# Attention beside a gated feed-forward block on one core: the row maxima reach the query rows by VectorE and DRAM instead of TensorE, and a tanh moves one mark forward

## The chip, the cores and the metric

The kernel runs on 1 core of one Trainium2 chip. The metric is device time in microseconds (us), the median of several runs. Five engines work side by side, each with its own in-order instruction stream: TensorE (PE in the profile, with its weight loads listed apart as PEld), VectorE (DVE), ScalarE (ACT), GpSimd (POOL) and SyncE (SP), whose queue issues all of this kernel's DMAs. PE writes its sums into PSUM banks; DVE and ACT read them there.

## The reference, cut to what matters

```python
def _A_ref(x, wqkv, wo):                       # S 2048, D 576, H 32, Dh 18
    q, k, v = ...
    scores = jnp.einsum("bhqd,bhkd->bhqk", q, k) * (Dh ** -0.5)
    p = softmax(scores, axis=-1)
    o = jnp.einsum("bhqk,bhkd->bhqd", p, v)
    return o.transpose(0, 2, 1, 3).reshape(B, S, D) @ wo

def _B_ref(x, w_gate, w_up, w_down):           # F 4608
    return (gelu(x @ w_gate, approximate=True) * (x @ w_up)) @ w_down

xn = layernorm(x, axis=-1, eps=1e-5)
out = x + _A_ref(xn, wqkv, wo) * silu(_B_ref(xn, w_gate, w_up, w_down))
```

Everything is float32. The softmax subtracts the maximum of each query's row, and the change is about how that maximum gets to where it is subtracted.

## The kernel before, in words

A prologue normalizes x, computes q, k and v and writes them to DRAM, each number as a rounded high part and a low remainder. The main part is one long hand-written PE order (PE alone is scheduled by hand; the order on the other engines and on the DMA queue is a planner's, which keeps to the hand-made order where the code asks for it). An epilogue projects the attention output and combines.

**Sections.** The main part consists of 144 sections (`section`). Section n computes one 128-wide slice of gate and up (`gate_up`: `pg` and `pu`, 27 pairs of matmuls that run side by side on the two 64-row halves of PE), and between those pairs the attention's matmuls are spread. The first ten sections (`FIRST`) lead in; the 128 sections of `ATT` carry the attention. After the matmuls of a section come, on odd attention sections, the products with the values (`values`), and on even ones the down projection of the slices two sections back (`half_downs`). After 36 sections a block of 512 tokens is complete and the next block's x is loaded (a block change).

**Attention units.** A unit is 4 heads by 512 queries, 32 units in all, 4 sections each. Two matmuls serve a unit's scores. `max_mm` computes scores with queries on the partitions (`pm`), and a `TENSOR_REDUCE` on DVE keeps each row's maximum (L701). It runs 40 slots, that is 5 sections, ahead of `score_mm`, which computes the scores again with keys on the partitions (`pe`), already with the maximum subtracted, and ACT takes the exponential (L736). The subtraction costs no operation of its own: the query tiles (`QS`, rows of 64 per head) have spare rows from `MROW` (54) on that meet rows of ones in the key tiles, and the negated maximum, as a high and a low part, is written into two of those rows by DMA. So the maximum, which DVE has with queries on partitions, has to become a row along the free axis. That is what the change touches:

- `max_neg` (L703 on, called when a unit's last maximum is done, in every fourth section, always an even one): the four parts of each maximum are reduced and negated (`nm`, L706), and split into high and low (L708, L709) in a constant tile `m2_ident`, which also holds an identity.
- `max_end` (L711 on): called in the middle of that section's down projection (`half_downs`, `middle`). PE multiplies the two 64-row halves of the parts with the identity (L717), which transposes them into two PSUM banks (tags `m` and `f`); ACT copies them out (`mr`, L720); eight DMAs on the SP queue write the rows of the query tiles (L725).
- The unit's first `score_mm` comes two sections after `max_neg`.

**The down projection in halves.** `half_downs` makes 8 sums of 128x288 (`py`, k = 0 to 7), each of 12 matmuls, 6 on the lower and 6 on the upper 64 rows of PE. Two lanes run side by side, 48 steps of two matmuls: lane 1 does k = 0 to 7 in order, lane 0 does k = 6, 7, then 0 to 5. So sum k = 0 is begun in steps 0 to 5 on lane 1 and ended in steps 12 to 17 on lane 0, and so on. When lane 1 has finished its half of a sum (k = 0 to 5, every six steps), a tiny ACT instruction (`mark`, L471) follows it, and lane 0's half waits for the mark. A finished sum is added to `Y` by DVE (`add_down`, L455), which frees its PSUM bank. Banks are handed out by tag in turn, `bank("mmsmfmss"[k])`, with 2 of tag `f`, 3 of `m` and 3 of `s`: sum k = 5, begun at step 30 on lane 1, is the fourth of tag `m` and takes the bank of k = 0. The bank of k = 4 is that of `pg`.

**The activation.** `activate` makes the gated value of a section: ACT squares `pg` (L430), DVE forms the polynomial (L431), then `times` (ACT copies `pu`, L435; DVE multiplies by `pg`, L438) and `rest` (ACT's tanh, L441; DVE's product, L444). In sections with a down projection `times` and `rest` are popped out of a list by it: `times` behind the mark of k = 0, `rest` behind the mark of k = 2. `finish` then splits the result on POOL (`hh`, `hl`, L108 and L110), and POOL goes on to split the next weights.

**The DMA queue.** SP issues the keys (`KS`, L667, 12 DMAs a section), the weights (L128), the values, the query rows and the small transfers of the softmax sums in the planner's order; an issue that has to wait holds up all behind it.

Of the kernel before, what the change touches and what calls it, by code (L numbers as in the profile page):

```python
# [8 lines left out]
F32 = mybir.dt.float32  # L9
F32R = mybir.dt.float32r  # L10
AF = mybir.ActivationFunctionType
# [30 lines left out]
FIRST = (0, 0, 4, 4, 4, 4, 6, 6, 6, 6)  # L42
ATT = range(len(FIRST), len(FIRST) + NU * NA)
MROW = 3 * DH
MH = 32
MW = 72
NK = KT + 1
BANKS = {"f": 2, "m": 3, "s": 3}
EPS = 1e-5
# [5 lines left out]
def f(ap):  # L55
    return ap.bitcast(F32)
# [13 lines left out]
def kernel(ctx: ExitStack, tc: tile.TileContext, x, wqkv, wo, w_gate, w_up, w_down, out):  # L70
# [14 lines left out]
    rT = dram.tile([H, S], F32, name="rT")  # L85
    oN = dram.tile([D, S], F32, name="oN")
    ys = dram.tile([S - TB, D], F32, name="ys")
    zq = dram.tile([HR - MROW, TB], F32, name="zq")
    xhs = [dram.tile([2, D, TB], F32, name=f"xhs{b}") for b in range(NB)]

    m2_ident = const.tile([P, 2 * MH + HR], F32R, name="m2_ident")
    M2 = m2_ident[:, 0:2 * MH].rearrange("p (i c) -> p i c", c=MH)
    identr = m2_ident[:, 2 * MH:2 * MH + HR]
    all_t = slice(0, TB)

    def after(what, before):
# [62 lines left out]
    with tc.tile_pool(name="pro", bufs=1) as pro, tc.tile_pool(name="pps", bufs=1, space=PSUM) as pps:  # L159
        ident = pro.tile([P, P], F32, name="ident")  # L160
        make_identity(nc, ident)
        for a in (0, HR):
            nc.gpsimd.tensor_copy(identr[a:a + HR], ident[a:a + HR, a:a + HR])

        def load_rest(c0, n, keep=lambda i: i):

# [234 lines left out]
    def kept(i):  # L401

        if FF["keep"]:
            tc.keep_in_program_order(i)
        return i
# [21 lines left out]
    def activate(pg, pu, early):  # L427

        t1 = ffn.tile([P, TB], F32, name="t1", bufs=2)
        kept(nc.scalar.activation(t1, pg, AF.Square))  # L430
        kept(nc.vector.scalar_tensor_tensor(t1, t1, 1.0 / GC, pg, op0=ALU.add, op1=ALU.mult))  # L431
        t2 = ffn.tile([P, TB], F32, name="t2", bufs=1) if early else None

        def times(behind=None):
            one = nc.scalar.activation(t2, pu, AF.Copy)  # L435
            if behind:
                no_sync(one, behind, "a mark first")
            nc.vector.tensor_tensor(t2, t2, pg, op=ALU.mult)  # L438

        def rest(behind=None):  # L440
            tanh = kept(nc.scalar.activation(t1, t1, AF.Tanh, scale=GC * GS))  # L441
            if behind:
                no_sync(tanh, behind, "a mark first")
            kept(nc.vector.scalar_tensor_tensor(t1, t1, 1.0, t2 if early else pg, op0=ALU.add, op1=ALU.mult))  # L444
            if not early:
                kept(nc.vector.tensor_tensor(t1, t1, pu, op=ALU.mult))

        return t1, [times, rest] if early else [rest]

    def add_down(b, r, py, Y, j, c):  # L450
        yy = Y[:, j, 288 * c:288 * c + 288]
        if r == 0:
            nc.vector.tensor_copy(yy, py)
        else:
            kept(nc.vector.tensor_tensor(yy, py, yy, op=ALU.add))  # L455
        if b == NB - 1 and r == NR - 1:
            FF["final"](Y, j, c)

    DOWN = [(a, w, g) for g in range(G) for a, w in ((0, 0), (0, 1), (1, 0))]

# [11 lines left out]
        after(it, one)  # L472
        return it

    def half_downs(b, r, hs, wd, Y, middle=None):

        m = len(DOWN)
        sums = [(j, c) for j in range(TB // P) for c in range(2)]  # L480
        low = len(sums) - 2
        pys, seen = {}, {}

        def downs_of(a, ks):
            for k in ks:
                for i in range(m):
                    def step(k=k, i=i):
                        j, c = sums[k]
                        fresh = k not in pys
                        if fresh:  # L490
                            pys[k] = bank("mmsmfmss"[k])
                        begun = a if k < low else 1 - a
                        one = down_product(pys[k], hs, wd, j, c, i, slice(HR * a, HR * a + HR), fresh,
                                           begun == 0 and i == m - 1)
                        if begun == 0 and i == 0 and k in seen:
                            after(one, seen[k])
                        if i == m - 1:
                            if begun == 0:
                                add_down(b, r, pys[k], Y, j, c)
                            elif a == 1:  # L500
                                seen[k] = behind(one)
                                if k in (0, 2) and FF["rest"]:
                                    FF["rest"].pop(0)(seen[k])
                    yield step

        n = range(len(sums))
        rows = [*downs_of(0, n[low:]), *downs_of(0, n[:low])], [*downs_of(1, n)]
        for i, both in enumerate(zip(*rows, strict=True)):
            for half in both if i < low * m + m else both[::-1]:
                half()  # L510
            if middle and i == (low - 1) * m + 1:
                middle()

    def down(b, r, hs, wd, Y, js, once):
        last = len(DOWN) - 1
        if once:
            if js[0] == 0:
                half_downs(b, r, hs, wd, Y, FF.pop("middle", None))
        else:
            for j in js:  # L520
                for c in range(2):
                    py = bank("sf"[c if b == NB - 1 and r == NR - 1 else 0])
                    for i in range(len(DOWN)):
                        down_product(py, hs, wd, j, c, i, start=(i == 0), stop=(i == last))
                    add_down(b, r, py, Y, j, c)
        if b < NB - 1 and r == NR - 1:
            for j in js:
                kept(nc.sync.dma_start(ys[b * TB + j * P:b * TB + (j + 1) * P, :], Y[:, j]))
# [117 lines left out]
    with tc.tile_pool(name="att", bufs=1, reuse_waits="tile") as att:  # L646
        VS = [att.tile([P, VC * VW + 32 - DH - 1], F32, name=f"VS{i}") for i in range(VB)]
        for i, kk in enumerate(KS):
            for r in range(2):
                (nc.vector, nc.gpsimd)[i % 2].memset(f(kk[r]), 1.0)  # L650
        nc.vector.memset(f(M2), 0.0)
        for vv in VS:
            nc.vector.memset(vv[:, VC * VW:], 0.0)

# [22 lines left out]
        QS, MX, ACC, PT, NM, DEN, PIECE = {}, {}, {}, {}, {}, {}, {}  # L677

        def load_q(u, rs=(0, 1)):
            j, g = divmod(u, NQ)  # L680
# [21 lines left out]

        def max_neg(u, keep=lambda i: i):  # L703

            nm = att.tile([P, 4 * QD], F32, name="nm", bufs=1)
            keep(nc.vector.tensor_reduce(nm, MX[u].rearrange("p a t c -> p (a t) c"), axis=AX.X, op=ALU.max, negate=True))  # L706
            NM[u], m2 = u, M2
            nc.vector.tensor_copy(m2[:, 0, 0:4 * QD], nm)  # L708
            nc.vector.tensor_tensor(m2[:, 1, 0:4 * QD], nm, f(m2)[:, 0, 0:4 * QD], op=ALU.subtract)  # L709

        def max_end(u, tags="mf"):  # L711

            NM.pop(u)
            pms = [ps.tile([P, TB], F32, name="pm", tag=tag, bufs=BANKS[tag])[0:MW, 0:HR] for tag in tags]
            for a, pm in enumerate(pms):
                rr = slice(HR * a, HR * a + HR)
                nc.tensor.matmul(pm, m2_ident[rr, 0:MW], identr[rr], start=True, stop=True)  # L717
            mr = att.tile([P, TB // 2], F32, name="mr", tag="piece", bufs=2)[:, 0:P]
            for a, pm in enumerate(pms):
                nc.scalar.activation(mr[0:2 * MH, HR * a:HR * a + HR], pm[0:2 * MH], AF.Copy)  # L720
            for a in range(QD):
                for i in range(2):
                    row = 64 * (a % 2) + MROW + i
                    c = MH * i + 4 * a
                    nc.sync.dma_start(f(QS[u, a // 2])[row:row + 1, :], mr[c:c + 4, :])  # L725

        def score_mm(u, i, a, tag="s"):

# [89 lines left out]
        for n, m in enumerate(FIRST):  # L818
            none = [lambda: None]
            lead = [lambda s=s: lead_pair(s) for s in range(slot, slot + m)]  # L820
            if 0 in NM:
                lead.insert(1, lambda: max_end(0, "ms"))
            section((n == 2) * 5 * none + lead + (m > 0 and n != 2) * none, "s" if n == 1 else "f", lead_raw)
            if slot + m >= NS > slot:
                max_neg(0, tc.keep_in_program_order)
            slot += m
            while n > 1 and chunk < KB and chunk * SLOTS <= slot + SLOTS:
                load_k(chunk, tc.keep_in_program_order)
                chunk += 1
            if n == 3:  # L830
                load_q(1)
            if n >= len(FIRST) - 2:
                load_v(n - len(FIRST) + 2)
            downs()
            finish(cut=split_ap)
        for n in range(NU * NA):
# [13 lines left out]
            um, im = divmod(s0 + LEAD + SLOTS, NS)  # L850
            if im == 0 and um <= NU:
                max_neg(um - 1)
                FF["middle"] = lambda u=um - 1: max_end(u)
            if i % 2:
                for kt in range((i - 1) * VC, (i + 1) * VC):
                    values(u, kt)
# [192 lines left out]
```

## Time and profile before

| | us |
|---|---|
| median of 3 runs | 2559.11 (2557.44 to 2561.36) |
| the profiled execution's own time | 2559.35 |
| its span, first to last instruction | 2557.3 |
| PE busy with matmuls | 2544.7 |
| DVE busy | 1948.9 |
| ACT busy | 1563.7 |
| POOL busy | 1321.8 |
| DVE's maxima (L701), 2048 times | 1250.0 |
| DVE's sums into Y (L455), 544 times | 228.8 |

The busy time of an engine counts time in which at least one of its instructions runs; matmuls overlap, since each starts before the one ahead of it has drained. The time of 2559.35 us has 2.05 us around the span. In views by time, a row gives the start, the duration, the engine, the source line, the operation, output and inputs, the shape, the count where equal rows are merged, and in brackets the idle time before it with what ended it.

### The profile page before, as it was taken

The numbers are of one execution on the slowest core, as the hardware profiler recorded it, in microseconds if no ns is written. First come the engines' busy times: TensorE is split into PE (matmuls) and PEld (weight loads), VectorE is DVE, ScalarE is ACT, GpSimd is POOL, SyncE is SP. The second block draws the span as 40 slices with busy tenths as digits, with TensorE's granted clock in tenths as the row PEclk, the third lists the DMA queues.
The fourth block names the chain that finished last, engine by engine and source line by source line (L and its number), as shares of the span: only waits on it lengthen the run. The fifth ranks groups of instructions, "written<-read, shape, count | busy, mean of one in ns | idle before, by whom it ended". The sixth has DMA issues, their size and how long they took to land.

```text
span 2557.3 us, 63358 instructions
## 1 busy us (share of the span) xinstructions
PE 2544.7 (100%) x24038; PEld 1977.7 (77%) x24038; DVE 1948.9 (76%) x3468; ACT 1563.7 (61%) x3114; POOL 1321.8 (52%) x1449
## 2 busy tenths in 40 slices
PE   9999999999999999999999999999999999999999
PEld 8888877777777777777777777777777777777798
DVE  5316978888888888888888888888888888886277
ACT  3223467666667666667666667666666666676612
POOL 2117645555565555444556554554446555555575
PEclk9999999999999999999999999999999999999999
DMA  8876343444464444444455443444446444443483
GB/s 267 270 238 161 94 106 92 108 105 110 109 155 118 106 103 111 112 112 111 109 122 141 115 108 101 109 104 109 109 99 159 111 109 109 111 107 99 113 245 105
DMA packets 391006, 324.98 MB, mean 127 GB/s; under 512 B 108704, under 2 KB 301504, under 8 KB 390704
## 3 DMA queue, kind: packets, MB, share of 16 engines
q1 hardware_dynamic: 390704, 320.94, 48.6%
q8 instruction: 191, 3.13, 0.5%
q14 instruction: 111, 0.91, 0.1%
HBM read 266.10 MB, written 54.18 MB: 125 GB/s over the span
## 4 chain that ended last, share of the span: by engine, by line
PE 95%; DVE 2%; ACT 2%; DMA 1%; issue 0%; POOL 0%; SPq 0%; ACTq 0%; DVEq 0%; POOLq 0%
PE pg L417 31%; PE acc L770 17%; PE py L466 16%; PE pm L700 9%; PE pe L735 9%; PE po L184 7%; PE pu L417 3%; PE po L909 2%; DVE t L444 1%; ACT pT L736 1%; ACT t L441 1%; DVE Y L455 0%; DMA xd<-xhs 0%; DVE mx L701 0%; PE pt L245 0%; PE pm L717 0%
## 5 line engine op out<-in xcount | busy, mean ns | idle before, releaser
L736 ACT ACTIVATE pT<-pe 128x512 f32<-128x512 f32 x2048 | 1151.3, 598 | 370.3 <-PE pm L700 266.2
L701 DVE TENSOR_REDUCE mx<-pm 128x1 f32<-128x512 f32 x2048 | 1250.0, 680 | 151.9 <-PE pm L700 149.3
L417 PE MATMUL pu<-xd,wh 64*128 64x512 f32 x2592 | 929.3, 390 | 0.6 <-POOL xd L148 0.5
L417 PE MATMUL pg<-xd,wh 64*128 64x512 f32 x2592 | 928.7, 390 | 0.0
L700 PE MATMUL pm<-KS,q 64*128 64x512 f32 x2048 | 782.5, 387 | 0.0
L735 PE MATMUL pe<-q,KS 64*128 64x512 f32 x2048 | 776.8, 387 | 0.0
L417 PEld LDWEIGHTS pg<-xd,wh 64*128 64x128 f32 x2592 | 476.4, 184 | 127.5 <-issue 26.1
L417 PE MATMUL pu<-xd,wl 64*128 64x512 f32 x1296 | 501.5, 387 | 0.0
L417 PE MATMUL pg<-xd,wl 64*128 64x512 f32 x1296 | 501.4, 387 | 0.0
L417 PEld LDWEIGHTS pu<-xd,wh 64*128 64x128 f32 x2592 | 476.8, 184 | 4.2 <-POOL xd L148 1.5
L770 PE MATMUL acc<-pT,VS 128*32 128x512 f32 x4096 | 452.8, 594 | 0.0
L110 POOL TENSOR_TENSOR wl<-raw,wh 128x384 fp32r<-128x384 f32 x432 | 433.9, 1018 | 13.7
L700 PEld LDWEIGHTS pm<-KS,q 64*128 64x128 f32 x2048 | 374.3, 184 | 35.0 <-DVE mx L701 3.8
L735 PEld LDWEIGHTS pe<-q,KS 64*128 64x128 f32 x2048 | 370.1, 184 | 27.1
L108 POOL TENSOR_SCALAR hh<-t 128x512 fp32r<-128x512 f32 x128 | 79.2, 619 | 579.8 <-DVE t L444 565.7
L770 PEld LDWEIGHTS acc<-pT,VS 128*32 128x32 f32 x4096 | 127.3, 110 | 289.9 <-issue 278.6
L466 PE MATMUL py<-dh,hl 64*128 64x288 f32 (+1 forms) x2160 | 344.2, 295 | 0.0
L466 PE MATMUL py<-dh,hh 64*128 64x288 f32 (+1 forms) x2160 | 343.0, 292 | 0.3
L466 PE MATMUL py<-dl,hh 64*128 64x288 f32 (+1 forms) x2160 | 341.5, 292 | 0.0
L108 POOL TENSOR_SCALAR wh<-raw 128x384 fp32r<-128x384 f32 x432 | 217.7, 516 | 130.2 <-PE pu L417 79.2
L455 DVE TENSOR_TENSOR Y<-py,Y 128x288 f32<-128x288 f32 x544 | 228.8, 452 | 58.6 <-PE py L466 51.9
L417 PEld LDWEIGHTS pg<-xd,wl 64*128 64x128 f32 x1296 | 238.6, 184 | 38.2
(123 smaller groups left out, 3067.0 us busy)
## 6 DMA issues: line engine op xcount, KB each, us to landing
KS<-qk SPq DMA_DIRECT2D x1536, 36.0 KB
raw<-in_B_w_gate_dram SPq DMA_DIRECT2D x144, 288.0 KB
raw<-in_B_w_up_dram SPq DMA_DIRECT2D x144, 288.0 KB
raw<-in_B_w_down_dram SPq DMA_DIRECT2D x67, 576.0 KB
VS<-vs SPq DMA_DIRECT2D x128, 152.0 KB
qk<-t SPq DMA_DIRECT2D x72, 256.0 KB
q<-qk SPq DMA_DIRECT2D x384, 36.0 KB
xx<-in_A_x_dram SPq DMA_DIRECT2D x32, 288.0 KB
```

The lines of the kernel that those rows point to most:

```text
L108: first = nc.gpsimd.tensor_scalar(hi, raw, 1.0, 1.0, op0=ALU.mult, op1=ALU.mult)
L110: low_part[:] = [keep(nc.gpsimd.tensor_tensor(lo, raw, f(hi), op=ALU.subtract))]
L184: nc.tensor.matmul(o, st, m, start=(i == 0), stop=(i == len(terms) - 1))
L417: nc.tensor.matmul(o, w[1 + wp][k][rr, c, :], xd[xp][k][rr, c, :], start=(i == 0), stop=(i == len(terms) - 1))
L455: kept(nc.vector.tensor_tensor(yy, py, yy, op=ALU.add))
L466: return nc.tensor.matmul(py, hs[g][a][rr, j * P:(j + 1) * P], wd[w][rr, g, 288 * c:288 * c + 288], start=start, stop=stop)
L700: nc.tensor.matmul(pm, QS[u, r][rr, t * P:(t + 1) * P], KS[(u * NA + c) % KB][r][rr, :], start=True, stop=True)
L701: nc.vector.tensor_reduce(MX[u][:, 2 * r + a, t, c:c + 1], pm, axis=AX.X, op=ALU.max)
L735: nc.tensor.matmul(pe, KS[(u * NA + c) % KB][r][rr, t * P:(t + 1) * P], QS[u, r][rr, :], start=True, stop=True)
L736: nc.scalar.activation(PT[u, kt][:, 2 * r + a, :], pe, AF.Exp, scale=SCALE)
L770: nc.tensor.matmul(ACC[u][32 * a:32 * a + 32, :], VS[(u * NA + c) % VB][:, v:v + 32], pt[:, a, :], start=first, stop=last, skip_group_chec ...
L909: nc.tensor.matmul(po, parts_of(b, j)[x_][:, k, :], OW[w][c][k], start=(i == 0), stop=(i == len(OUT) - 1))
```

## The change

The maxima's parts no longer pass through PE and ACT. `max_neg` puts high and low part side by side into a 128x32 tile `m2`, DVE transposes it in squares of 32 (`m2t`), and one DMA stores it to a DRAM tile `mT` of the unit. `max_rows` reads it back with eight DMAs, one for each row, each in 16 pieces of 32 numbers. It is called in the section after `max_neg`, but the planner puts its DMAs behind the twelve key loads of the section of `max_neg`. `max_end`, its 64 matmuls and 64 ACT copies, the identity and the place in the middle of the down projection go away; the transposes add 32 instructions on DVE and the stores 32 DMAs.

In the planned order, `mT`'s store stands between the eighth and the ninth key load, and the eight row loads right behind the twelfth. On DVE the transpose stands between L431 and L438.

The second part: `rest` is popped behind the mark of k = 1 instead of k = 2, except where the down projection is a block's last (`r == NR - 1`). There it stays at k = 2, and its DVE product is kept behind the sum of k = 0. Elsewhere the DVE order becomes L431, (transpose,) L438, L444, and then the eight sums; before, the sum of k = 0 stood ahead of L444.

```diff
-MH = 32
-MW = 72
+MH = 16
+SQ = 32
...
+    mT = [dram.tile([P, SQ], F32, name=f"mT{u}") for u in range(NU)]
...
-    m2_ident = const.tile([P, 2 * MH + HR], F32R, name="m2_ident")
-    M2 = m2_ident[:, 0:2 * MH].rearrange("p (i c) -> p i c", c=MH)
-    identr = m2_ident[:, 2 * MH:2 * MH + HR]
...
-        def rest(behind=None):
+        def rest(behind=None, evicted=None):
             tanh = kept(nc.scalar.activation(t1, t1, AF.Tanh, scale=GC * GS))
             if behind:
                 no_sync(tanh, behind, "a mark first")
-            kept(nc.vector.scalar_tensor_tensor(t1, t1, 1.0, t2 if early else pg, op0=ALU.add, op1=ALU.mult))
+            one = kept(nc.vector.scalar_tensor_tensor(t1, t1, 1.0, t2 if early else pg, op0=ALU.add, op1=ALU.mult))
+            if evicted:
+                no_sync(one, evicted, "a finished sum first")
...
-    def half_downs(b, r, hs, wd, Y, middle=None):
+    def half_downs(b, r, hs, wd, Y):
...
-        pys, seen = {}, {}
+        pys, seen, evicted = {}, {}, None
+        late = 2 if r == NR - 1 else 1
...
                             if begun == 0:
-                                add_down(b, r, pys[k], Y, j, c)
+                                evicted = add_down(b, r, pys[k], Y, j, c)
                             elif a == 1:
                                 seen[k] = behind(one)
-                                if k in (0, 2) and FF["rest"]:
-                                    FF["rest"].pop(0)(seen[k])
+                                if k in (0, late) and FF["rest"]:
+                                    FF["rest"].pop(0)(seen[k], evicted if k == 2 else None)
...
-            if middle and i == (low - 1) * m + 1:
-                middle()
...
-            nm = att.tile([P, 4 * QD], F32, name="nm", bufs=1)
+            nm = att.tile([P, MH], F32, name="nm", bufs=1)
+            m2 = att.tile([P, 2 * MH], F32R, name="m2", bufs=1)
+            m2t = att.tile([P, SQ], F32, name="m2t", bufs=1)
             keep(nc.vector.tensor_reduce(nm, MX[u].rearrange("p a t c -> p (a t) c"), axis=AX.X, op=ALU.max, negate=True))
-            NM[u], m2 = u, M2
-            nc.vector.tensor_copy(m2[:, 0, 0:4 * QD], nm)
-            nc.vector.tensor_tensor(m2[:, 1, 0:4 * QD], nm, f(m2)[:, 0, 0:4 * QD], op=ALU.subtract)
-
-        def max_end(u, tags="mf"):
-
-            NM.pop(u)
-            pms = [ps.tile([P, TB], F32, name="pm", tag=tag, bufs=BANKS[tag])[0:MW, 0:HR] for tag in tags]
-            for a, pm in enumerate(pms):
-                rr = slice(HR * a, HR * a + HR)
-                nc.tensor.matmul(pm, m2_ident[rr, 0:MW], identr[rr], start=True, stop=True)
-            mr = att.tile([P, TB // 2], F32, name="mr", tag="piece", bufs=2)[:, 0:P]
-            for a, pm in enumerate(pms):
-                nc.scalar.activation(mr[0:2 * MH, HR * a:HR * a + HR], pm[0:2 * MH], AF.Copy)
+            nc.vector.tensor_copy(m2[:, 0:MH], nm)
+            nc.vector.tensor_tensor(m2[:, MH:2 * MH], nm, f(m2)[:, 0:MH], op=ALU.subtract)
+            nc.vector.transpose(m2t, f(m2))
+            nc.sync.dma_start(mT[u], m2t)
+
+        def max_rows(u):
+
+            parts = mT[u].rearrange("(b i a t) r -> i a t b r", i=2, a=QD, t=4)
             for a in range(QD):
                 for i in range(2):
-                    row = 64 * (a % 2) + MROW + i
-                    c = MH * i + 4 * a
-                    nc.sync.dma_start(f(QS[u, a // 2])[row:row + 1, :], mr[c:c + 4, :])
+                    row = HR * (a % 2) + MROW + i
+                    nc.sync.dma_start(f(QS[u, a // 2])[row:row + 1, :].rearrange("o (t b r) -> o t b r", t=4, r=SQ),
+                                      parts[i:i + 1, a])
...
             if slot + m >= NS > slot:
                 max_neg(0, tc.keep_in_program_order)
+                max_rows(0)
...
                 max_neg(um - 1)
-                FF["middle"] = lambda u=um - 1: max_end(u)
+                at(n + 1, 0, max_rows, um - 1)
```

More of the change, by code (lines that the diff above doesn't have):

```diff
@@ L161 @@
         make_identity(nc, ident)
-        for a in (0, HR):
-            nc.gpsimd.tensor_copy(identr[a:a + HR], ident[a:a + HR, a:a + HR])
         def load_rest(c0, n, keep=lambda i: i):
@@ L432, in activate, with times @@
         t2 = ffn.tile([P, TB], F32, name="t2", bufs=1) if early else None
-        def times(behind=None):
+        def times(behind=None, _=None):
             one = nc.scalar.activation(t2, pu, AF.Copy)
@@ L452, in add_down @@
         if r == 0:
-            nc.vector.tensor_copy(yy, py)
+            one = nc.vector.tensor_copy(yy, py)
         else:
-            kept(nc.vector.tensor_tensor(yy, py, yy, op=ALU.add))
+            one = kept(nc.vector.tensor_tensor(yy, py, yy, op=ALU.add))
         if b == NB - 1 and r == NR - 1:
             FF["final"](Y, j, c)
+        return one
     DOWN = [(a, w, g) for g in range(G) for a, w in ((0, 0), (0, 1), (1, 0))]
@@ L487, in step @@
                     def step(k=k, i=i):
+                        nonlocal evicted
                         j, c = sums[k]
@@ L517, in down @@
             if js[0] == 0:
-                half_downs(b, r, hs, wd, Y, FF.pop("middle", None))
+                half_downs(b, r, hs, wd, Y)
         else:
@@ L650 @@
                 (nc.vector, nc.gpsimd)[i % 2].memset(f(kk[r]), 1.0)
-        nc.vector.memset(f(M2), 0.0)
         for vv in VS:
@@ L675, in load_v @@
                                   vs[c * TB:(c + 1) * TB, QD * g:QD * (g + 1), :].rearrange("(t p) h d -> p t (h d)", p=P))
-        QS, MX, ACC, PT, NM, DEN, PIECE = {}, {}, {}, {}, {}, {}, {}
+        QS, MX, ACC, PT, DEN, PIECE = {}, {}, {}, {}, {}, {}
         def load_q(u, rs=(0, 1)):
@@ L820 @@
             lead = [lambda s=s: lead_pair(s) for s in range(slot, slot + m)]
-            if 0 in NM:
-                lead.insert(1, lambda: max_end(0, "ms"))
             section((n == 2) * 5 * none + lead + (m > 0 and n != 2) * none, "s" if n == 1 else "f", lead_raw)
```

## The prediction

> **What bounds the kernel now.** First the page: busy times, and the chain that ended last.
>
> ```profile
> span 2557.3 us, 63358 instructions
> PE 2544.7 (100%) x24038; PEld 1977.7 (77%) x24038; DVE 1948.9 (76%) x3468; ACT 1563.7 (61%) x3114; POOL 1321.8 (52%) x1449
> PE 95%; DVE 2%; ACT 2%; DMA 1%; issue 0%; POOL 0%; SPq 0%; ACTq 0%; DVEq 0%; POOLq 0%
> ```
>
> PE is busy all the time and is 95% of the chain. Only two things can then move the end: PE instructions that go away, and moments in which PE stands still. DVE, ACT, POOL and SP matter only where they make PE wait. So next: does PE stand still around the removed matmuls? The view of the tile `m_ident`, and of the marks:
>
> ```profile
> L717 PEld LDWEIGHTS pm<-m_ident x64: 136/136/137, 288.8 to 2352.3; 64*72 64x72 f32 x64
> L709 DVE TENSOR_TENSOR m_ident<-nm,m_ident x32: 174/176/1211, 287.5 to 2349.1; 128x16 fp32r<-128x16 f32 x32
>   DVE Y L455: 13.1, 33
> L471 ACT ACTIVATE mark<-mark 128x1 f32<-128x1 f32 x378 | 76.9, 203 | 117.6 <-PE py L466 107.0
> ```
>
> There are 64 loads, a pair for each of 32 units, and before them PE sat idle for 13.1 us, waiting for a sum of DVE: the transposes want two PSUM banks in the middle of a down projection, and the `m` bank is still waiting to be added to `Y`. The 378 marks are 6 for each of 63 down projections in halves; 31 of these hold a transpose (the first unit's stands in the lead), 32 do not. Now PE's timeline through one of each kind, first the one with:
>
> ```profile
> 1210.85 0.29 PE L466 MATMUL py<-dh,hh 64*128 64x288 f32 x2
> ...
> 1215.38 0.25 PE L717 MATMUL pm<-m_ident 64*72 64x64 f32 x2
> ...
> 1217.68 0.39 PE L417 MATMUL pg<-xd,wh 64*128 64x512 f32 x1
> ```
> ```profile
> 1177.72 0.29 PE L466 MATMUL py<-dh,hh 64*128 64x288 f32 x2
> ...
> 1184.08 0.39 PE L417 MATMUL pg<-xd,wh 64*128 64x512 f32 x1
> ```
>
> From the first sum to the next section's first matmul it is 6.83 us with the transpose and 6.36 without: 0.47 us for each.
>
> **The change, part by part.** *The matmuls of L717 go.* 31 x 0.47 = 14.6 us of PE time. The pair in the lead stands between matmuls that need no bank of it, and I count it at nothing. The 64 copies on ACT (L720) go too, which PE never waited for. At least the idle 13.1 us is gone, at most 14.6 plus a few tenths.
>
> *DVE gets a transpose, and the first sum moves behind the tanh's product.* This is where something can be given back, since DVE's first sum frees the bank of k = 5. The three views of the section at 1210.85, DVE, ACT and the weight load of step 30 (1210.85 plus 30 steps of 0.13 us is its matmul at 1214.82, the load stands one step ahead):
>
> ```profile
> 1211.97 0.17 DVE L708 CAST m_ident<-nm 128x16 fp32r<-128x16 f32 x1
> 1212.18 0.18 DVE L709 TENSOR_TENSOR m_ident<-nm,m_ident 128x16 fp32r<-128x16 f32 x1
> 1212.28 0.68 DVE L431 SCALAR_TENSOR_TENSOR t<-t,pg 128x512 f32<-128x512 f32 x1
> 1212.87 0.68 DVE L438 TENSOR_TENSOR t<-t,pg 128x512 f32<-128x512 f32 x1
> 1213.47 0.45 DVE L455 TENSOR_TENSOR Y<-py,Y 128x288 f32<-128x288 f32 x1
> 1214.27 0.69 DVE L444 SCALAR_TENSOR_TENSOR t<-t,t 128x512 f32<-128x512 f32 x1 [0.35 <-ACT t L441]
> 1214.88 0.81 DVE L455 TENSOR_TENSOR Y<-py,Y 128x288 f32<-128x288 f32 x2
> ```
> ```profile
> 1212.70 0.20 ACT L471 ACTIVATE mark<-mark 128x1 f32<-128x1 f32 x1
> 1213.51 0.20 ACT L471 ACTIVATE mark<-mark 128x1 f32<-128x1 f32 x1 [0.62 <-PE py L466]
> 1213.62 0.62 ACT L441 ACTIVATE t<-t 128x512 f32<-128x512 f32 x1
> ```
> ```profile
> 1214.68 0.19 PEld L466 LDWEIGHTS py<-dh,hh 64*128 64x128 f32 x2
> ```
>
> No row shows a transpose on DVE. The nearest are the small ones of the same unit. An instruction that nobody waits for takes a place of 0.10 us (L709 to L431, 1212.18 to 1212.28), one whose result the next needs 0.21 us (L708 to L709). The transpose reads twice as many numbers and is independent of L438 behind it: I take 0.12 us, and keep 0.10 and 0.25 as ends.
>
> The Trainium skill, VectorE: DVE Perf Modes, section The TRN2 errata, gives 58 cycles plus one per element at 0.96 GHz from SBUF to SBUF, which would be 0.09 us for 32 elements, and says beside it that the fixed part measures nearer 150 cycles, which would be 0.19 us; the two L708 and L709 rows last 0.17 and 0.18 us for 16 elements and side with the second. By it the loss worked out below would be 4.8 instead of 2.8 us.
>
> Now the new order. The tanh may start behind the mark of 1212.70, but L431 ends only at 1212.96; the tanh takes 0.62 us and would be done at 1213.6 or a little later. L438 ends at 1213.55 + 0.12 = 1213.67, and L444, which needs both, starts 0.03 us behind (as it starts at 1214.27 behind the tanh that ended at 1214.24): 1213.70 to 1214.39. The sum of k = 0 overlaps its end by 0.08 us (1214.88 against 1214.96) and takes 0.45: 1214.31 to 1214.76, where it now ends at 1213.92. How soon PE follows, a block change shows, where the same sum is late already:
>
> ```profile
> 1347.83 0.44 DVE L455 TENSOR_TENSOR Y<-py,Y 128x288 f32<-128x288 f32 x1
> ```
> ```profile
> 1348.15 0.36 PEld L466 LDWEIGHTS py<-dh,hh 64*128 64x128 f32 x2
> 1348.33 0.29 PEld L466 LDWEIGHTS py<-dl,hh 64*128 64x128 f32 x2
> ```
>
> The sum ends at 1348.27, and the load of the lane that begins k = 5 comes 0.06 us later, at 1348.33 instead of 1348.15. So in the changed order the load of 1214.68 would come at about 1214.81, 0.13 us late. Some of that is inside the step by which a load runs ahead; I take 0.10 us of PE time. Sections of this kind that are not a block's last: 28 of the 31, so 2.8 us given back. With a transpose of 0.25 us the load is 0.26 us late, and 28 x 0.22 = 6.2 us are given back; with nothing lost in the load's lead, 0.
>
> In the 32 sections without maxima, the same steps:
>
> ```profile
> 1179.49 0.69 DVE L438 TENSOR_TENSOR t<-t,pg 128x512 f32<-128x512 f32 x1
> ```
> ```profile
> 1179.56 0.20 ACT L471 ACTIVATE mark<-mark 128x1 f32<-128x1 f32 x1
> ```
> ```profile
> 1181.55 0.19 PEld L466 LDWEIGHTS py<-dh,hh 64*128 64x128 f32 x2
> ```
>
> The tanh starts 0.11 us behind its mark (1213.51 to 1213.62 above), at 1179.67, and ends at 1180.29; L438 is done at 1180.18, so L444 runs from 1180.32 to 1181.01, the sum from 1180.93 to 1181.38, and with 0.06 us the bank is free at 1181.44, 0.11 us before the load of 1181.55. Nothing is lost, and nothing gained either: the product that is done earlier goes to POOL, whose next hidden values are wanted a section later. If that cover of 0.11 us were gone, a tenth in 32 sections is 3 us.
>
> The three block changes keep the old order, and get the transpose ahead of the late sum: 0.1 us each if it is quick, about 1.0 if it is stretched as L709 sometimes is (longest 1211 ns, median 176). I take 0.3, so 0.9 us in all, and keep 3.0 as the end.
>
> *The DMAs.* SP gets one issue more, and it stands between key loads:
>
> ```profile
> 1209.00 5.10 SPq L667 DMA_DIRECT2D KS<-qk  x12
> ...
> 1216.02 5.05 SPq L725 DMA_DIRECT2D q<-mr  x8
> ```
> ```profile
> 1175.65 0.57 SPq L778 DMA_DIRECT2D sT<-accs  x1
> ...
> 1177.90 0.54 SPq L799 DMA_DIRECT2D sums<-sT  x1
> ```
> ```profile
> 1219.28 0.39 PE L735 MATMUL pe<-q,KS 64*128 64x512 f32 x1
> ```
>
> The store waits for the transpose, so until about 1213.1, and holds the last four key loads behind it, then issues in about 0.57 us (as the store of `sT`). The last keys are issued by 1215.2 instead of 1214.1. Those four belong to the second tile of keys, first used at 1219.28, or 1218.8 with PE 0.47 us earlier: 3.6 us for the landing. The bound for a landing is the pair at 1175.65: a read of what a store of the same size class wrote is issued 2.25 us after the store. So the keys are hidden by over a microsecond. The eight rows wait for the store to land, from 1213.1 + 2.25 = 1215.4, and at about 0.6 us each are out by 1220.3 where they end at 1221.07 now, so the weights behind them come no later. The rows themselves are wanted two sections later, some 15 us. I cost it all at nothing; if the cover were gone, each microsecond is 31 us.
>
> **The sum.** 2559.35 - 14.6 + 2.8 + 0.9 = 2548.45 for an execution like the profiled one; the median of the runs stands 0.24 us under it, so 2548.2 us.
>
> **Rivals.** *A: the bank is free in time after all.* The 0.13 us vanish in the load's lead. 2559.1 - 14.6 = 2544.5 us. For it: the delay is no longer than one step of PE. Against: at 1348.33 PE does show the wait.
>
> *B: slower, by the transpose.* DVE's small operations are stretched at times: L709 has a longest of 1211 ns against a median of 176, and no row names the cause. A transpose of that length in 28 sections makes the sum of k = 0 late by 1.2 us in each: 28 x 1.2 - 14.6 = 19 us more, 2578 us. It decides from about 0.6 us on, where 28 x 0.5 eats the gain. Against it: if the cause is POOL's work beside it, POOL is idle at that moment:
>
> ```profile
> 1215.05 0.62 POOL L108 TENSOR_SCALAR hh<-t 128x512 fp32r<-128x512 f32 x1 [8.90 <-DVE t L444]
> ```
>
> *C: slower, by the queue.* A landing of 5 us instead of 2.25 makes PE wait 1.4 us for keys in each unit: 31 x 1.4 = 43 us, 2588 us. It passes the gain from a landing of 4.1 us on.
>
> *D: no change; the stall is taken up again.* DVE's last four sums and the next maxima follow; if these set the pace, the next section waits for its banks instead, and 2559 us stays. For it: DVE is busy without a break there. Against: those sums wait for PE's products, so they move with it, and the section without a transpose runs on without a stall.
>
> **How the numbers follow.** The forecast 0.66, A 0.16, B 0.06, C 0.05, D 0.07. The range reaches from A (2544.5, less a few tenths for the lead) to the long transpose and three stretched ones (2559.1 - 14.6 + 6.2 + 3.0 = 2553.7) and half a microsecond beyond: 2543.8 to 2554.2. Within 0.2%, about 5 us, a measurement of this kernel cannot tell a change. Faster: forecast and A, 0.82. Same: D, 0.07. Slower: B and C, 0.11.
>
> **What would show it.** No row of L717's kind, and 6.36 to 6.5 us from the first `py` to the next section's `pg` in every down projection; a wait of PE's loads for DVE's sum of about 0.1 us in 28 sections; a transpose of 0.1 to 0.25 us; no wait of PE for a DMA. The prediction is wrong if PE waits for keys or query rows, if the transpose is stretched, or if PE stands still at the next section's start.

## The result, and the profile after

The changed kernel takes 2547.11 us (median of 6 runs, 2546.57 to 2547.97) against 2560.16 us before (6 runs, 2557.44 to 2561.37): a ratio of 0.995, 95% interval 0.9937 to 0.9963. It is faster, by 13 us; 2548.2 was forecast. As a gain, 10.9 us were forecast and 13.05 measured; half of that difference is that these six runs of the kernel before are 1.05 us slower than the 2559.1 from which the forecast started. The profiled execution took 2547.22 us, with this on its page: the span, the busy times, and the shares of the chain that ended last.

```profile
span 2545.4 us, 63167 instructions
PE 2538.4 (100%) x23974; PEld 2008.4 (79%) x23974; DVE 1950.4 (77%) x3499; ACT 1555.1 (61%) x3050; POOL 1320.7 (52%) x1447
PE 98%; ACT 1%; DVE 0%; DMA 0%; SPq 0%; issue 0%; ACTq 0%
```

PE's share of the chain rose from 95 to 98%, and DVE's fell from 2% to nothing: waits of PE for DVE went, not only the 64 matmuls (24038 - 23974). The new instructions, in the view of the tile `m2t` (duration in ns: shortest, median, longest):

```profile
L709 DVE STREAM_TRANSPOSE m2t<-m x32: 196/204/205, 289.1 to 2338.3; 128x32 f32<-128x32 f32 x32
L710 SPq DMA_DIRECT2D mT<-m2t x32: 319/349/474, 289.3 to 2338.5; - x32
```

PE's timeline (start, duration, operation), one down projection with maxima, and then one without:

```profile
1207.59 0.29 PE L465 MATMUL py<-dh,hh 64*128 64x288 f32 x2
...
1213.97 0.39 PE L413 MATMUL pg<-xd,wh 64*128 64x512 f32 x1
...
1214.11 0.39 PE L413 MATMUL pu<-xd,wh 64*128 64x512 f32 x1
```
```profile
1174.49 0.29 PE L465 MATMUL py<-dh,hh 64*128 64x288 f32 x2
...
1180.85 0.39 PE L413 MATMUL pg<-xd,wh 64*128 64x512 f32 x1
```

Without maxima nothing changed: 6.36 us. With maxima it is 6.38 us on the one lane of PE and 6.52 us on the other, where it was 6.83. The two lanes, which work on half of the rows each, no longer run level at the end, so one of them stood still for a step. The same section on DVE, on ACT, and in PE's weight loads shows where:

```profile
1209.02 0.68 DVE L427 SCALAR_TENSOR_TENSOR t<-t,pg 128x512 f32<-128x512 f32 x1
1209.61 0.20 DVE L709 STREAM_TRANSPOSE m2t<-m 128x32 f32<-128x32 f32 x1
1209.74 0.64 DVE L434 TENSOR_TENSOR t<-t,pg 128x512 f32<-128x512 f32 x1
1210.49 0.69 DVE L440 SCALAR_TENSOR_TENSOR t<-t,t 128x512 f32<-128x512 f32 x1
1211.10 1.18 DVE L453 TENSOR_TENSOR Y<-py,Y 128x288 f32<-128x288 f32 x3
```
```profile
1209.73 0.63 ACT L437 ACTIVATE t<-t 128x512 f32<-128x512 f32 x1
```
```profile
1211.42 0.36 PEld L465 LDWEIGHTS py<-dh,hh 64*128 64x128 f32 x2
1211.61 0.29 PEld L465 LDWEIGHTS py<-dl,hh 64*128 64x128 f32 x2
```

(L427, L434, L437, L440, L453 and L465 are L431, L438, L441, L444, L455 and L466 of before.) The three sums in a row begin at 1211.10; the first of them ends at 1211.55, and the second lane's load of step 30 follows at 1211.60: the row of 1211.42 holds both lanes' loads, of 0.18 us each, the one at 1211.42 and the other done at 1211.78. So it stands 4.02 us behind the first matmul; in the kernel before it was at 3.84.

At the block changes, the three sections with maxima took 6.83, 7.28 and 7.65 us before, and take 6.36 us each now. PE's timeline at the second of them:

```profile
1340.36 0.29 PE L465 MATMUL py<-dh,hh 64*128 64x288 f32 x2
...
1346.72 0.39 PE L413 MATMUL pg<-xd,wh 64*128 64x512 f32 x1
```

There is one new wait, in the lead, where the first unit's keys come. SP's timeline after, then before:

```profile
289.31 0.35 SPq L710 DMA_DIRECT2D mT<-m2t  x1
290.78 5.40 SPq L718 DMA_DIRECT2D q<-mT  x8
296.23 4.40 SPq L665 DMA_DIRECT2D KS<-qk  x12
```
```profile
289.51 5.26 SPq L725 DMA_DIRECT2D q<-mr  x8
294.87 4.61 SPq L667 DMA_DIRECT2D KS<-qk  x12
```

And the waits of 285 to 320 us after (what waited, for what; total us, times, longest), which before have no such row:

```profile
PEld pm L698 <- DMA KS<-qk: 0.9, 1, 0.9
```

The eight rows stand idle on SP for the store to land, from 289.66 to 290.78, the twelve key loads behind them go out 1.4 us later than before (296.23 against 294.87), and PE waits 0.9 us for them. The prologue ends at a different time in each execution, but this stretch does not vary with it: from the eighth to the ninth group of `py` matmuls in the lead (296.04 to 310.60 us here) it takes 13.4 us in the four profiles of this document without that wait, and 14.4 to 14.6 in the five with it.

In sum, over the profiled executions, in us of span (2557.3 to 2545.4, so 11.9):

| where | forecast | measured |
|---|---|---|
| 28 ordinary sections with maxima, from one section's start to the next's | 28 x (0.47 - 0.10) = 10.4 | 28 x 0.336 = 9.4 |
| 3 block changes | 3 x (0.47 - 0.3) = 0.5 | 0.47 + 0.92 + 1.29 = 2.7 |
| 32 sections without maxima | 0 | 0 |
| ahead of the first down projection in halves (343.43 against 344.54) | 0 | -1.1 |
| a wait for a new block's `xd`, below | 0 | 1.2 |
| the rest | 0 | -0.3 |
| sum | 10.9 | 11.9 |

The wait for `xd` stands in the kernel before between 1935 and 1946 us, in the waits of that stretch:

```profile
PEld pu L417 <- POOL xd L148: 1.5, 2, 0.9
```

The changed kernel has no such row for `pu` at that place. Of the versions below only E2 has it, for 0.4 us; E6, which also keeps PE's transposes, has none. The kernel before was profiled once, so whether all its executions wait there stays open, and I don't count it as the change's work.

### The profile page after: what moved, and what is told of

Its sections match the earlier page's. It is cut to its first block, busy times and chain, and to the rows that moved or that the text cites. A ratio compares the mean times of both kernels' runs of the same rounds, so it can differ in the third digit from the quotient of the medians.

```text
span 2545.4 us, 63167 instructions
## 1 busy us (share of the span) xinstructions
PE 2538.4 (100%) x23974; PEld 2008.4 (79%) x23974; DVE 1950.4 (77%) x3499; ACT 1555.1 (61%) x3050; POOL 1320.7 (52%) x1447
## 4 chain that ended last, share of the span: by engine, by line
PE 98%; ACT 1%; DVE 0%; DMA 0%; SPq 0%; issue 0%; ACTq 0%
PE pg L413 29%; PE py L465 18%; PE acc L764 18%; PE pm L698 9%; PE pe L729 9%; PE po L180 7%; PE pu L413 6%; PE po L902 2%; ACT pT L730 1%; PE pt L241 0%; SPq L665 0%; DMA xx<-in_A_x_dram 0%; DVE bs L209 0%; ACT t L426 0%; DMA KS<-qk 0%
## 5 line engine op out<-in xcount | busy, mean ns | idle before, releaser
L465 PE MATMUL py<-dh,hh 64*128 64x288 f32 (+1 forms) x2160 | 360.3, 294 | 0.3
L465 PE MATMUL py<-dl,hh 64*128 64x288 f32 (+1 forms) x2160 | 358.7, 292 | 0.0
L465 PE MATMUL py<-dh,hl 64*128 64x288 f32 (+1 forms) x2160 | 358.3, 292 | 0.0
L453 DVE TENSOR_TENSOR Y<-py,Y 128x288 f32<-128x288 f32 x544 | 227.1, 452 | 59.8 <-PE py L465 52.7
```

Of the source, the lines that this page charges most:

```text
L453: one = kept(nc.vector.tensor_tensor(yy, py, yy, op=ALU.add))
L465: return nc.tensor.matmul(py, hs[g][a][rr, j * P:(j + 1) * P], wd[w][rr, g, 288 * c:288 * c + 288], start=start, stop=stop)
```

## The experiments

All but the last are medians of at least 5 runs, against the kernel before on the same chip (2559.24 us for E1, E2, E5 and E6, 2559.34 for E3, E4 and E8). E3, E4 and E8 ran on another chip than E1, E2, E5 and E6, and which chip the changed kernel had is not known. So where two versions are compared by a difference of their times, the profiles are the safer ground. From the start of the first down projection in halves to the start of the last one with maxima, which leaves out the prologue and the lead, they give:

| | us | less than before |
|---|---|---|
| before | 2004.4 | |
| the change | 1991.7 | 12.7 |
| E1, the route alone | 1988.3 | 16.1 |
| E2, the tanh alone | 1999.3 | 5.1 |
| E3, two transposes | 1998.4 | 5.9 |
| E4, the transpose behind the sum | 1989.6 | 14.8 |
| E5, E1 with the keys first | 1988.3 | 16.1 |
| E6, PE's transposes later | 1991.8 | 12.6 |
| E8, no exception | 1991.8 | 12.6 |

(About 1.2 us of each number in the last column is the wait for `xd` above, of which E2 gains only a part.)

My theory: the gain is the removed pair of L717 with its wait, and what is missing of it is lost since the first sum stands behind the tanh's product and the transpose, which frees the bank of k = 5 too late. The rival: the route by way of DRAM costs it (transpose, DMAs), or the two edits gain each a share.

**E1, the route alone.** The transpose and the DMAs stay; the tanh stays behind the mark of k = 2 everywhere, as before.

```diff
-        late = 2 if r == NR - 1 else 1
+        late = 2
```

> The new way of the maxima alone: the tanh stays behind the mark of k = 2 in every down projection, with its product behind the sum of k = 0; the DMA queue's order is that of the changed kernel. Theory: the changed kernel loses 0.13 us in each of 28 down projections because its sum of k = 0 comes behind the tanh's product; with the old order the sum ends some 0.8 us earlier, the load of step 30 is on time, and 28 x 0.13 = 3.6 us come back: 2543.5 us, and 6.36 us per down projection of either kind. Rival: the earlier tanh is worth something elsewhere (POOL's hidden values, the next weights), then this is as slow as or slower than the changed kernel: 2547 us or more.

Measured: 2543.89 us (2543.83 to 2544.46), ratio 0.9937 (0.9924 to 0.9951). DVE's timeline in a section with maxima, and PE's:

```profile
1142.28 0.65 DVE L434 TENSOR_TENSOR t<-t,pg 128x512 f32<-128x512 f32 x1
1142.84 0.45 DVE L453 TENSOR_TENSOR Y<-py,Y 128x288 f32<-128x288 f32 x1
```
```profile
1140.12 0.29 PE L465 MATMUL py<-dh,hh 64*128 64x288 f32 x2
...
1146.49 0.39 PE L413 MATMUL pg<-xd,wh 64*128 64x512 f32 x1
```

The first sum ends 3.17 us behind the first matmul instead of 3.96, and PE does not wait for it: 6.37 us here, and a median of 6.36 both with and without maxima. So in the units the route by way of DRAM costs PE nothing, but for 0.1 us at one block change (below), and the new place of the tanh gives back 2547.11 - 2543.89 = 3.2 us, or 3.4 by the profiles. The same wait in the lead is here too (1.0 us for keys).

**E2, the tanh alone.** The kernel before with its transposes on PE, and the tanh's product ahead of the first sum as in the change (at block changes behind it, as there).

> The earlier tanh alone, the maxima still transposed by TensorE in the middle of the down projection. Theory: TensorE's transpose waits there for DVE's sum of k = 1; with the product ahead of both sums that sum ends about 0.2 us earlier (4.25 instead of 4.48 us behind the first matmul of the down projection), so the wait of 0.33 us shrinks to about 0.1, while step 30 loses a few hundredths for the sum of k = 0: 28 x 0.2 = 5 us faster than the kernel before, about 2555 us. Rival: both waits add up, and it is 2 to 4 us slower than before, about 2563 us; or the tanh's place does nothing: 2560 us.

```diff
+        late = 2 if r == NR - 1 else 1
...
-                                if k in (0, 2) and FF["rest"]:
-                                    FF["rest"].pop(0)(seen[k])
+                                if k in (0, late) and FF["rest"]:
+                                    FF["rest"].pop(0)(seen[k], evicted if k == 2 else None)
```

Measured: 2553.16 us (11 runs, 2551.98 to 2558.56), ratio 0.9978 (0.9969 to 0.9986). DVE's timeline and PE's:

```profile
1146.73 0.69 DVE L444 SCALAR_TENSOR_TENSOR t<-t,t 128x512 f32<-128x512 f32 x1
1147.34 1.20 DVE L457 TENSOR_TENSOR Y<-py,Y 128x288 f32<-128x288 f32 x3
```
```profile
1143.92 0.29 PE L469 MATMUL py<-dh,hh 64*128 64x288 f32 x2
...
1150.51 0.39 PE L417 MATMUL pg<-xd,wh 64*128 64x512 f32 x1
```

A gain of 6.1 us, from an edit that costs 3.2 with the other route. With the product out of the way, the sums of k = 0, 1 and 2 follow each other, and that of k = 1 ends at 4.24 us (median) instead of 4.48. That is the sum for which the transposes on PE wait; the section takes 6.59 instead of 6.83. The two edits attack the same idle time: 15.3 us for the route alone and 6.1 for the tanh alone, but some 13 for both (16.1, 5.1 and 12.7 by the profiles). What speeds up the old route delays the new one.

**E3, one transpose too many.** The changed kernel, with a second transpose of the same tile behind the first.

```diff
-            nc.vector.transpose(m2t, f(m2))
+            for _ in range(2):
+                nc.vector.transpose(m2t, f(m2))
```

> The changed kernel with DVE's transpose made twice in a row for each unit. Theory: the second takes a place of 0.1 us ahead of the sum of k = 0, the load of step 30 comes 0.28 instead of 0.18 us late, and each of 28 down projections loses 0.1 us more, the three at block changes nothing: 2547.1 + 2.8 = 2550 us, 6.5 to 6.6 us per down projection with maxima. Rival: the loss does not come from DVE's order, and nothing changes: 2547 us.

Measured: 2555.18 us (11 runs, 2554.55 to 2557.44), ratio 0.9984 (0.9975 to 0.9993), 8.1 us over the change. DVE's timeline and the weight loads (in brackets the idle time ahead, and what ended it):

```profile
1147.03 0.45 DVE L710 STREAM_TRANSPOSE m2t<-m 128x32 f32<-128x32 f32 x2
1147.40 0.64 DVE L434 TENSOR_TENSOR t<-t,pg 128x512 f32<-128x512 f32 x1
```
```profile
1149.26 0.18 PEld L465 LDWEIGHTS py<-dh,hh 64*128 64x128 f32 x1 [0.24 <-DVE Y L453]
```

The 2550 us that I expected were missed by 5 us, and the size of one term is why: I had expected 0.1 us for the second transpose and it takes 0.24. Both write the same tile, so the second probably waits for the first; no run has it write another tile. (L434 starts 0.37 us behind the pair, and 0.13 behind the single one above.) The load that waits stands 4.26 us behind the first matmul instead of 4.02, 0.24 later, and names its cause: the sum of L453. 28 x 0.24 = 6.7 us; 1.0 of the rest lies ahead of the first unit in this execution (345.50 against 344.54). So the mechanism is confirmed, at a higher price: from this point on each delay of DVE is one of PE's, nearly one for one.

**E4, the transpose behind the first sum.** The changed kernel, with the transpose moved from ahead of L434 to behind the sum of k = 0; its store then goes out behind all twelve key loads.

```diff
-            nc.vector.transpose(m2t, f(m2))
-            nc.sync.dma_start(mT[u], m2t)
+            def turn(behind=None):
+                one = nc.vector.transpose(m2t, f(m2))
+                if behind:
+                    no_sync(one, behind, "a finished sum first")
+                nc.sync.dma_start(mT[u], m2t)
...
+            else:
+                FF["turn"] = turn
...
+                                if k == 0 and "turn" in FF:
+                                    FF.pop("turn")(evicted)
```

> The changed kernel with DVE's transpose moved behind the sum of k = 0 of the same down projection; the store then stands behind all twelve key loads. Theory: the sum of k = 0 ends 0.1 us earlier, the load of step 30 is 0.08 us late instead of 0.18, and most of that is inside a load's lead: 28 x 0.1 = 2.8 us faster than the changed kernel, 2544.3 us. Rival: the later store delays the query rows and the weights behind them, and the time is 2547 us or more.

Measured: 2545.47 us (2545.01 to 2545.68), ratio 0.9945 (0.9932 to 0.9959). DVE's timeline and PE's:

```profile
1144.78 0.45 DVE L453 TENSOR_TENSOR Y<-py,Y 128x288 f32<-128x288 f32 x1
1145.15 0.20 DVE L713 STREAM_TRANSPOSE m2t<-m 128x32 f32<-128x32 f32 x1
```
```profile
1141.37 0.29 PE L465 MATMUL py<-dh,hh 64*128 64x288 f32 x2
...
1147.73 0.39 PE L413 MATMUL pg<-xd,wh 64*128 64x512 f32 x1
```

The load of step 30 is 0.08 us late instead of 0.18 (median 3.92), the section is back at 6.36 us on one lane and takes 6.43 on the other, and half of what E1 gains over the change is there (2.1 of 3.4 us by the profiles). That is 1.2 us short of the 2544.3 that I expected. The rest is the tanh's product by itself: that order costs about 0.03 us in most units even without the transpose ahead of it, and this execution began its units later than E1's as well (345.21 against 344.72).

**E5, the first unit's keys ahead of its rows.** E1, and in the lead the rows are read behind the key loads, not ahead of them.

```diff
                 max_neg(0, tc.keep_in_program_order)
-                max_rows(0)
...
+            if slot >= NS > slot - m:
+                max_rows(0)
```

> As the new way alone, and in the lead the first unit's eight row loads are issued behind the next keys instead of ahead of them. Theory: in the lead of the changed kernel the row loads wait for their store to land, hold up twelve key loads, and TensorE waits 0.9 us for keys; that wait goes: about 1 us under the run with the new way alone, 2542.5 us, and no wait of TensorE for keys at 302 us in the profile. Rival: that wait came from the chance of one execution, then the two are equal.

Measured: 2543.22 us (2542.41 to 2544.73), ratio 0.9934 (0.9922 to 0.9947). SP's timeline in the lead:

```profile
289.46 0.35 SPq L710 DMA_DIRECT2D mT<-m2t  x1
289.85 4.29 SPq L665 DMA_DIRECT2D KS<-qk  x12
294.24 5.40 SPq L718 DMA_DIRECT2D q<-mT  x8
```

The keys fill the time in which the store lands, and the waits of this stretch have no row of PE for keys any more. The first down projection in halves begins 1.2 us earlier than in E1 (343.55 against 344.72), and the span is 2540.9 against 2542.1 us. The medians differ by 0.7 us, with ranges that overlap, so that this saves a microsecond is shown by the profiles, not by the times. Its median is the lowest here, and its runs all lie below those of both kernels.

**E6, the transposes on PE, later.** The kernel before, with its `middle` six steps later (behind step 37 instead of 31; the text below says five, and 36), where the bank of k = 1 is free.

```diff
-            if middle and i == (low - 1) * m + 1:
+            if middle and i == low * m + 1:
```

> The kernel before, with TensorE's transposes of the maxima moved five steps later in the down projection (behind step 36 instead of 31), where the sum of k = 1 has been added to Y. Theory: of the 0.47 us that a transpose costs, 0.33 are the wait for that sum and only 0.13 the matmuls: 31 x 0.33 = 10 us faster than before, about 2550 us, without any way by DRAM. Rival: the matmuls themselves, which break the run of paired sums, are the cost, and it stays at 2560 us.

Measured: 2547.09 us (2546.8 to 2547.52), ratio 0.9949 (0.9937 to 0.9962). PE's timeline:

```profile
1206.78 0.29 PE L466 MATMUL py<-dh,hh 64*128 64x288 f32 x2
...
1211.82 0.19 PE L717 MATMUL pm<-m_ident 64*72 64x64 f32 x2
...
1213.25 0.39 PE L417 MATMUL pg<-xd,wh 64*128 64x512 f32 x1
```

The section takes 6.47 us: the pair itself costs 0.11 and its wait had cost 0.36. One changed line is as fast as the whole change (12.6 against 12.7 us by the profiles). I had expected 2550: 0.03 us more per unit account for 0.9 us of the difference, and two block changes for most of the rest, which took 7.28 and 7.65 us before and take 6.47 here.

**E8, no exception at block changes.** The changed kernel with the early tanh in every section (`late = 1`). One execution.

> The changed kernel without the exception at block changes: the tanh behind the mark of k = 1 and its product ahead of the sums there too. Theory: at the three block changes DVE is late already, and a sum of k = 0 behind the product comes 0.2 to 0.7 us late: these three down projections take 6.5 to 7.0 us instead of 6.36, at most 2 us in all, not to be told from the time, only from the profile. Rival: they take 6.36 us, and the exception does nothing.

It took 2549.3 us, of which 2.0 over the change lie ahead of the first unit (346.53 against 344.54), in the prologue. The three block changes take 6.38 us on the one lane and 6.51 to 6.52 on the other where the exception gives 6.36: they behave as the other sections with maxima, at the low end of the 6.5 to 7.0 us I expected, and no small operation was stretched there in this execution. From section to section the exception is worth 0.4 us in all, too little to be seen in a time.

## Why the prediction was right

**The pairs of L717: right.** 6.83 us became 6.36 wherever nothing else came in (E1), so 0.47 for each of 31. E6 splits it: 0.36 is the wait for a bank, 0.11 the work. The total idle of 13.1 us which the profile of before put down to DVE fits: 31 x 0.36 = 11.2, and more at the block changes.

**The transpose: right in its place, not in its next step.** I took 0.12 us in a range of 0.10 to 0.25. It moved L434's end by 0.09 us (median 2.80 against 2.71). But the product L440 then started 0.10 us behind L434 and not 0.03, since it waits here for L434's result, where my 0.03 came from a wait for ACT. So the first sum ends at 3.96 us where I had 3.91, and the load is 0.18 us late instead of 0.13.

**The loss in the 28 sections: right in kind, an eighth to a quarter too small.** 0.10 us each were forecast. From section to section 0.34 is gained instead of 0.47, so 0.13 is lost, 28 x 0.13 = 3.6 us instead of 2.8; the 28 sections of E1 and of the change differ by 3.5 us, and the times of the two by 3.2. The lead of the weight loads hid less than I thought: of 0.18 us late, 0.13 are lost, one whole step of a lane.

**The sections without maxima: right.** The first sum ends at 3.66 us there (1181.38 - 1177.72 was worked out), the load stays at 3.84, and nothing is lost.

**The block changes: wrong.** I forecast a loss of 0.9 us against the full gain, and there was none. The transpose was not stretched. DVE's small copy and subtraction still can be, and at the second block change of the changed kernel the copy is; POOL's timeline there, and DVE's:

```profile
1341.05 1.01 POOL L108 TENSOR_TENSOR wl<-raw,wh 128x384 fp32r<-128x384 f32 x1
```
```profile
1341.49 0.61 DVE L707 CAST m<-nm 128x16 fp32r<-128x16 f32 x1
```

It lasts 0.61 us instead of 0.17 and moves the sum of k = 0 from 3.17 to 3.60 us behind the first matmul. But with the sum ahead of L440, the old order that the change keeps here, the bank of k = 5 is wanted at 3.84 only, and the section takes 6.36 us all the same. In the kernel before, PE's transposes wanted the sum of k = 1 and had no such reserve: there a stretch went straight into 7.28 and 7.65 us. E6, where the pair comes later, has one too (first sum at 3.86 us instead of 3.08 at the third block change) and stays at 6.47. Of the gain of 2.7 us, 3 x 0.47 = 1.4 are the pairs, and 1.3 the stretches that no longer reach PE. The 1.3 are the reserve's work, and partly chance: at the first and the third block change nothing was stretched in this execution (first sums at 3.16 and 3.17 us), and a longer stretch passes the reserve. E1, with the same order at block changes, shows that at its second one: the subtraction lasts 0.96 us, the first sum ends at 3.95, and from this down projection to the next it takes 33.25 us instead of 33.13.

**The DMAs: right in the units, wrong in the lead.** In the units SP's timeline is as forecast, only earlier:

```profile
1209.84 0.35 SPq L710 DMA_DIRECT2D mT<-m2t  x1
1210.24 1.66 SPq L665 DMA_DIRECT2D KS<-qk  x4
1211.99 3.88 SPq L718 DMA_DIRECT2D q<-mT  x6
```

The rows go out right behind the fourth key load, since four key loads cover the landing. In the lead there is nothing between the store and the rows, and what I had as rival C (the queue makes PE wait for keys) happens there once: PE waits 0.9 us, and the lead is 1.1 us longer. The prediction named a wait of PE for keys as a sign that it is wrong, and in this one place it was. I had looked at the queue in a unit and had counted the lead at nothing; E5 shows that the order there was the cause.

So the forecast came within 1.1 us of the median because its misses (1.0 lost in the units and 1.1 in the lead that I had not counted, 2.2 gained at the block changes and 1.2 for `xd`) have both signs. The mechanism was right; that the number came so close is partly luck.

**The rivals.** A (the bank is free in time) is what E1 has, without the early tanh. D (the stall comes back later) did not occur: the section without a transpose stayed at 6.36 and the chain has no DVE left. B (a stretched transpose) did not occur in 32 of 32: its longest is 205 ns.

## What to carry to other kernels

A small operation in the middle of a matmul stream can cost much more than its own work, by the wait for the buffer that it needs (here 0.36 us of waiting for 0.11 of work): before moving it to another engine, try it a few steps later (E6). Two edits which remove the same wait do not add, and one of them can turn into a loss once the other has taken the wait away: measure each alone (E1, E2). A read behind a store holds up all that is queued behind it, so put independent loads between them (E5).

## What the runs showed of the hardware

*DVE's small copy and subtraction from SBUF to SBUF were stretched to the end of POOL's instruction; the transpose was not.* In the kernel before, POOL's and DVE's timelines at the longest L709:

```profile
287.39 1.29 POOL L115 TENSOR_TENSOR hl<-t,hh 128x512 fp32r<-128x512 f32 x1 [1.79 <-ACT hh L114]
```
```profile
287.50 1.21 DVE L709 TENSOR_TENSOR m_ident<-nm,m_ident 128x16 fp32r<-128x16 f32 x1
```

The subtraction, 0.18 us otherwise, ends at 288.71, 0.03 us behind the end of POOL's instruction that was running when it began (288.68). The copy of 1341.49 above ends at 1342.10, and POOL's instruction at 1342.06. The Trainium skill, SBUF — State Buffer, section Who interferes with whom, states this: VectorE and GpSimd share a pair of ports; a VectorE operation with two inputs in SBUF contends for it with a GpSimd instruction that reads SBUF, and so does a copy or cast in a two-port mode; whichever begins first has the pair for its whole instruction, and the other is blocked. Both cases agree with it, though no run shows in which mode the copy runs. Nor are they the only ones: in the nine profiles 28 of the 576 copies and subtractions last over 0.2 us, and each of the 28 begins while an instruction of POOL runs and ends 0.02 to 0.04 us behind the end of one. Of the other 548, all but two begin while POOL is idle. The transpose has one input, and in E4 it runs beside POOL; POOL's timeline there, and DVE's:

```profile
1211.29 0.62 POOL L106 TENSOR_SCALAR hh<-t 128x512 fp32r<-128x512 f32 x1 [8.29 <-DVE t L440]
```
```profile
1211.48 0.20 DVE L713 STREAM_TRANSPOSE m2t<-m 128x32 f32<-128x32 f32 x1
```

It begins and ends within POOL's instruction and takes its 0.20 us, so in 28 units of E4, and once in E5. So rival B rested on a likeness that does not hold. That POOL is the cause was read from coinciding ends; no run took its work away.

*A transpose of 128x32 numbers* lasts 0.20 us, and DVE's next independent instruction is 0.09 us later for it; a second one into the same tile costs 0.24 us (E3).

*The store of 16 KB to DRAM had landed within 1.5 us:* from the store's issue at 289.31 to the issue of the first row that waits for it, 290.78. I had used 2.25.
